# An SSD scan fused with a SiLU feed-forward block: a new order for the first fifty microseconds

## The chip, the cores and the metric

The kernel runs on one core of a Trainium2 chip. The metric is the device time of one execution in microseconds (us); three executions of the kernel before are known, and their median is compared. The engines are named as in the profile: PE is TensorE (PEld its weight loads), DVE VectorE, ACT ScalarE, POOL GpSimd, SP the queue that issues most DMAs. A DMA issued by POOL goes through another queue than those of SP.

## What is computed

Two blocks follow each other. The first is a Mamba-2 state-space scan with batch 4, 8 heads, 768 positions, head size 32 and state size 16; the second a feed-forward block with SiLU on the 3072 x 256 result. Cut to what matters:

```python
log_a = np.log(np.clip(a, 1e-06, 1.0))
for c in range(nc):                                   # chunks of 32 positions
    cum = np.cumsum(la, axis=-1)
    L = np.exp(cum[:, :, :, None] - cum[:, :, None, :]) * causal
    M = np.einsum('bhin,bhjn->bhij', Cc, Bc) * L
    y = np.einsum('bhij,bhjd->bhid', M, xc) + np.einsum('bhin,bhnd->bhid', Cc, state) * np.exp(cum)[..., None]
    state = np.exp(np.sum(la, -1))[:, :, None, None] * state + (decayed sum of B x over the chunk)
x = attn_out.transpose(0, 2, 1, 3).reshape(B * S, H * D)   # 3072 x 256
h = x @ w_in                                               # 256 x 2048
return (h * (1.0 / (1.0 + np.exp(-h)))) @ w_out            # 2048 x 256
```

## The kernel before

The work on tokens is cut into twelve *units* of 256 positions (three to a batch), each in four chunks of 64. The weights come in sixteen *blocks* of 128 x 512: 0 to 7 of w_in, 8 to 15 of w_out. Blocks are counted from zero here and in the code, so the "blocks six, seven" of the change's short name are blocks 5 and 6 of this text.

The weights arrive as pairs of 32-bit words (`load_w`, a tile `raw`, one of six buffers of the pool `quad`), and are made into float32 on the chip. `w_size(n)` on ACT writes `wu` with an Abs (L189) and `wv` with a scaled copy (L192). `w_bits(n)` on DVE clamps `wu` (a Max and a Min, L203), shifts it (L205) and puts the sign into `wv` (L206); POOL adds the two into the block `w` (L208). With `parts=2` the add is done in two halves, so that a product can start on the first.

For each unit the scan goes like this. `f_Ab` (unit 0 to 1) spreads the decays with PE into PSUM; `f_Ek` and `f_E1` make the decay matrix E from them by a running product on DVE (L358, the "scan"); later units load `ab` by DMA and scan from SBUF. `f_P` makes the prefix products `pfx` (L350) from `pz`, which POOL clips (`f_P0`, L346) for units 0 to 2. `f_TP` transposes B and C on PE (L396) and copies them out as BH (L399) and CT (L402) on ACT; `f_T` does it by a DVE transpose (L387); `f_T2` makes CE, two masked copies of C (L409, ACT). `f_B` and `f_C` weight B and C (L382, L413). `f_G` and `f_D0` are the score and state products on PE (L443, L429), `f_M` multiplies scores by E (L449, DVE), `f_S` carries the states on (L463, DVE), `f_SM` masks them (L470, ACT), `f_Y` makes y on PE (L483, L492), and `f_X` copies it out as `xf` (L502, ACT). E has one buffer, so a unit's scan waits for the y of the unit ahead; the PSUM tile `gy` (four banks) is one buffer too, and the banks of `acc` and `half` are two each.

Units 0 and 1 go through the feed-forward block in plain float32: `f_s1(u, j)` is unit u's product with block j into one of two PSUM halves `hp` (L532), with the Silu on ACT (L535, `gT`) that frees it; `f_s2(j)` is the product with block 8 + j (L545). From then on the units go in pairs through a split form (float32r, a high part, a low part and a cross term: L560, L568, L609, L610, L640), which fills the rest of the kernel. DMAs with accumulation from POOL make the low parts of the weights (L219, L229).

The order is written out by hand: the program runs under a manual schedule, so each engine and each queue executes its own operations in the order in which the Python code emits them, and waits by semaphores. The change lies in the list of calls from L697 to L782 and in the table `steps` (L841), which interleaves products, scans and weight blocks: an entry `(1, 4, "b7 r13 s8")` is unit 1's product with block 4, then `w_bits(7)`, the load of block 13 and `w_size(8)`; in "2:DSsM" the letters stand for parts of unit 2's scan (T: transposes and CE, P: prefix products, 1 and 2: the halves of E, B, C, D: the score and state products, S, s, M, Y: y and xf, x and a: loads). `busy` puts idle products on PE as filler.

Of the kernel before, what the change touches and what calls it, by code (L numbers as in the profile page):

```python
# [33 lines left out]
def kernel(  # L34
# [61 lines left out]
    def acc(name):  # L96
        return ps_a.tile([128, 512], FP32, name=name, tag="a")
# [18 lines left out]
    def load_n(u, i, q, ks=(0, 1)):  # L116
        b, t0 = at(u)
        if i == 1:
            if u not in tbc:
                tbc[u] = block("tbc0")[:, 0:256].rearrange("p (k h n) -> p k h n", k=2, h=H)  # L120
        elif u not in bn:
            bn[u] = (block("bn0")[:, 0:256].rearrange("p (k h n) -> p k h n", k=2, h=H) if u in (0, 1, 3) else
                     loads.tile([128, 2, H, N], FP32, name="bn"))
        for k in ks:
            q.dma_start(out=(bn, tbc)[i][u][:, k], in_=(B, C)[i][b, :, t0 + 128 * k:t0 + 128 * k + 128].rearrange("h p n -> p h n"))
# [49 lines left out]
    def load_w(n, q):  # L175
        j = n % 8
        src = wi[:, :, j * WF:(j + 1) * WF] if n < 8 else wo[:, 2 * j:2 * j + 2]
        if src.dtype == FP32:
            w32[n] = block("w32")
            q.dma_start(out=two(w32[n]), in_=src)  # L180
            return
        t = raw[n] = quad.tile([128, 2, WF, 2], U32, name="raw", tag="quad")
        q.dma_start(out=t.rearrange("p k f two -> p k (f two)"), in_=src.bitcast(U32))
# [10 lines left out]
    def w_bits(n, parts=1):  # L194
        if n in raw:
            u, v, hi = two(wu.pop(n)), two(wv.pop(n)).bitcast(U32), raw[n][:, :, :, 1]
            w32[n] = block("w32")
            for i in range(parts):
                fs = slice(WF // parts * i, WF // parts * (i + 1))
                if i == 0 or n == 0:  # L200
                    ws = fs if n == 0 else slice(0, WF)
                    ui = u[:, :, ws].bitcast(U32)
                    nc.vector.tensor_scalar(out=u[:, :, ws], in0=u[:, :, ws], scalar1=LEAST, scalar2=MOST,  # L203
                                            op0=ALU.max, op1=ALU.min)
                    nc.vector.tensor_scalar(out=ui, in0=ui, scalar1=3, scalar2=None, op0=ALU.logical_shift_left)  # L205
                    nc.vector.scalar_tensor_tensor(out=v[:, :, ws], in0=hi[:, :, ws], scalar=0x80000000, in1=v[:, :, ws],  # L206
                                                   op0=ALU.bitwise_and, op1=ALU.bitwise_or)
                nc.gpsimd.tensor_tensor(out=two(w32[n])[:, :, fs].bitcast(U32), in0=u[:, :, fs].bitcast(U32),  # L208
                                        in1=v[:, :, fs], op=ALU.add)
# [88 lines left out]
    def busy(n, small=0, t=None):  # L298
        t = half("zero") if t is None else t
        for i in range(n):  # L300
            nc.tensor.matmul(out=t, lhsT=idle[:, 0:128], rhs=idle, start=True, stop=True)
        for i in range(small):
            nc.tensor.matmul(out=t[:64, :64], lhsT=idle[:, 0:64], rhs=idle[:, 64:128], start=True, stop=True)
# [87 lines left out]
    def f_TP(u):  # L391

        d = new_dp(u)
        for i, t in enumerate((bn[u],) if u == 0 else (bn[u], tbc.pop(u))):
            for k in range(2):
                nc.tensor.transpose(out=d[:, 2 + i, 256 + 128 * k:384 + 128 * k],  # L396
                                    in_=t[:, k].rearrange("p h n -> p (h n)"), identity=ident)
        BH[u] = sc.tile([128, UT], FP32, name="bh")
        nc.scalar.activation(BH[u], d[:, 2, 256:512], AF.Copy)  # L399
        if u == 1:  # L400
            CT[u] = sc.tile([128, UT], FP32, name="ct")
            nc.scalar.activation(CT[u], d[:, 3, 256:512], AF.Copy)  # L402
        elif u > 0:
            CT[u] = d[:, 3, 256:512]

    def f_T2(u, e):
        if e == 0:
            CE[u] = sc.tile([128, 2, UT], FP32, name="ce")
        nc.scalar.activation(CE[u][:, e], CT[u], AF.Copy, scale=par[:, e:e + 1])  # L409
# [6 lines left out]
    def new_dp(u):  # L416
        if u not in DP:
            DP[u] = bank4()
        return DP[u]
# [285 lines left out]
    f_T(0, 1)  # L705
    for e in range(2):
        f_T2(0, e)
    load_w(4, nc.sync)
    load_ab(2, nc.sync)
    load_a(2)  # L710
    f_A1()
    f_Ek(0, 0, slice(4, 8))
    f_Ek(0, 1, slice(0, 4))
    busy(1, 10, new_dp(0)[:, 0])
    f_G(0)
    f_Ek(0, 1, slice(4, 8))
    f_B(0)
# [17 lines left out]
    busy(2)  # L735
    f_X(0)
    load_n(2, 1, nc.gpsimd, (0,))
    w_bits(1, 2)
    load_n(2, 1, nc.gpsimd, (1,))
    w_size(2)  # L740
    f_s1(0, 0)
    w_size(3)
    w_bits(2, 2)
    f_s1(0, 1)
    f_TP(1)
    for e in range(2):
        f_T2(1, e)
    f_Ek(1, 0)
    load_bcx(3, "c")
    for n in range(5, 7):  # L750
        load_w(n, nc.sync)
    f_Ek(1, 1)
    f_B(1, nc.gpsimd)
    f_s1(0, 2)
    w_bits(3, 2)
    w_size(4)
    f_P0(1, nc.gpsimd)
    f_G(1)
    f_D0(1)
    w_bits(4, 2)  # L760
# [5 lines left out]
    f_A2(True)  # L766
    f_A2(False)
    f_A3()
    load_w(7, nc.sync)
    load_pa(3, nc.sync)  # L770
    f_S(1)
    f_SM(1)
    f_M(1, 0)
    f_M(1, 1)
    f_s1(0, 3)
    w_size(5)
    f_s1(0, 4)
    f_Y(1)
    f_X(1)
    w_size(6)  # L780
    w_bits(5)
    load_n(3, 0, nc.gpsimd)  # L782

    def stage(u, what):
        for c in what:
            if c == "L":
                load_unit(u)
            elif c == "a":
                load_ab(u + 1, nc.sync)
            elif c == "x":  # L790
                load_x(u, nc.gpsimd)
            elif c == "T":
                if 0 < u < UPB:
                    f_TP(u)
                else:
                    f_T(u, 0)
                    f_T(u, 1)
                f_T2(u, 0)
                f_T2(u, 1)
            elif c == "P":  # L800
                f_P(u)
            elif c in "12":
                f_E1(u, int(c) - 1, 2)
            elif c == "B":
                f_B(u)
            elif c == "C":
                f_C(u)
            elif c == "D":
                f_G(u)
                f_D0(u)  # L810
            elif c == "M":
                f_M(u, 0)
                f_M(u, 1)
            elif c == "S":
                f_S(u)
            elif c == "s":
                f_SM(u)
            elif c == "Y":
                f_Y(u)
                f_X(u)  # L820
            elif c == "h":
                f_xh(u)
            elif c == "l":
                f_xl(u)
            elif c == "d":
                f_xd(u)
# [4 lines left out]
    def todo(text):  # L831

        for step in text.split():
            if ":" in step:
# [3 lines left out]
            n = int(step[1:].split(".")[0])  # L838
            {"b": w_bits, "s": w_size, "h": w_h, "l": w_l, "d": w_d, "v": partial(w_d, vector=True), "m": f_s2, "p": s1_d, "r": load_r}[step[0]](n)

    steps = ((1, 0, "2:PT1"), (1, 1, "2:C2Ba r8 r9 r10"), (1, 2, "3:x b6 r11 s7"), (1, 3, "2:DSsM r12"),  # L841
             (1, 4, "b7 r13 s8"), (0, 5, "3:T s9"), (1, 5, "2:Y b8 r14"), (0, 6, "3:1PC s10"),
             (1, 6, "b9 r15 3:2B s11 h0 l0"), (0, 7, "2:h s12"), (1, 7, "3:D b10 3:SsM"))
    for u, j, text in steps:
# [119 lines left out]
```

## Time and profile before

| what | us |
|---|---|
| median of three executions (333.96, 334.64, 336.03) | 334.64 |
| the profiled execution's own time | 334.75 |
| its span, from the first to the last instruction | 333.0 |
| clock granted to PE | 1.00 |
| DVE, ACT and POOL busy, share of the span | 76%, 66%, 28% |

How to read it: the timeline view gives, for each row, the start in the span, the time, the engine, the line, the operation with its tiles, and how many were merged; a bracket at the end gives the idle time of the engine before the row and what released it. Rows of issued DMAs (`DMA_DIRECT2D`) give the time of the issue, not of the transfer; the trace gives the time to landing for those of POOL. The chain of waits follows the work that ended last backwards, to what released each step. The DMA share is the mean busy share of the core's sixteen DMA engines.

Some rows of the first 50 us: unit 0's y ends at 13.62 and unit 1's at 29.89; unit 1's scans on DVE run from 18.34 to 20.66 behind blocks 1 and 2, beside POOL's adds of block 2 (18.73 to 20.16); block 5's DVE operations run from 30.36 to 32.96, unit 2's first scan from 33.91 to 36.14; SP issues blocks 5 and 6 at 26.09, the write of a_in at 32.44, block 7 at 34.02, unit 3's pz at 34.53, its ab at 37.61, and blocks 8 to 15 from 38.96 to 53.5.

### The profile page before, as it was taken

The page shows a single profiled execution, that of the slowest core. Times are in us where ns is not written, and L with a number is a line of the kernel's source. Part 1 is how long each engine was busy: PE and PEld are TensorE (multiplying, and loading weights), DVE is VectorE, ACT ScalarE, POOL GpSimd, SP SyncE. Part 2 cuts the span into 40 slices and gives each one's busy share as a digit, 9 for nine tenths or more (in the row PEclk, how much of TensorE's full clock was granted, in tenths as well). Part 3 has the DMA queues.
Part 4 walks back from the last instruction along what each step waited for, and adds up shares of the span by engine and source line. Part 5 has one row for each costly group of instructions (what it writes and reads, how often), then busy time and mean ns, then how long its engine had stood idle before and what let it go on. Part 6 is the DMA issues. An engine that isn't in the chain of part 4 may idle for free.

```text
span 333.0 us, 7980 instructions
## 1 busy us (share of the span) xinstructions
PE 322.2 (97%) x3219; PEld 260.3 (78%) x3221; DVE 253.3 (76%) x413; ACT 220.4 (66%) x422; POOL 92.5 (28%) x96
## 2 busy tenths in 40 slices
PE   8986989999999999999999999999999999999995
PEld 4565877888878778778778778778778778899995
DVE  7897979986876987996875996875996863484443
ACT  3665558687488898666767676767666756656661
POOL 6779735477011222231202230202240202000000
PEclk9999999999999999999999999999999999999999
DMA  6966796867893683164510254510253000012001
GB/s 138 291 172 194 196 368 212 161 111 126 147 172 76 116 150 63 49 110 90 107 31 0 54 106 93 112 23 0 60 101 64 2 2 0 0 27 39 0 2 63
DMA packets 79700, 31.87 MB, mean 96 GB/s; under 512 B 63168, under 2 KB 70080, under 8 KB 79664
## 3 DMA queue, kind: packets, MB, share of 16 engines
q1 hardware_dynamic: 73856, 24.42, 31.8%
q0 software_dynamic: 3440, 6.56, 10.5%
q10 hardware_dynamic: 2368, 0.39, 0.6%
q8 instruction: 25, 0.41, 0.5%
q14 instruction: 11, 0.09, 0.1%
HBM read 22.79 MB, written 3.32 MB: 78 GB/s over the span
## 4 chain that ended last, share of the span: by engine, by line
PE 88%; DMA 8%; ACT 2%; SPq 1%; issue 0%; DVE 0%
PE hp L568 23%; PE hp L560 11%; PE oa L609 9%; PE oa L610 9%; PE b L640 9%; PE oa L545 8%; PE hp L532 3%; DMA a_first<-ach 3%; PE b L635 2%; PE b L618 2%; PE oa L618 2%; DMA raw<-in_moe_w_out_dram 2%; PE gy L492 2%; PE gy L443 2%; DMA ab<-a_first 2%; PE gy L483 2%
## 5 line engine op out<-in xcount | busy, mean ns | idle before, releaser
L562 ACT ACTIVATE hp<-hp 128x512 f32<-128x512 f32 x80 | 46.6, 582 | 70.4 <-PE hp L560 70.3
L582 DVE TENSOR_TENSOR gl<-g,gh 128x512 fp32r<-128x512 f32 x62 | 42.7, 689 | 50.8 <-ACT gh L578 47.8
L568 PE MATMUL hp<-xh,wh 128*128 128x512 f32 x160 | 65.4, 409 | 0.0
L586 DVE SCALAR_TENSOR_TENSOR gd<-gh,g 128x512 fp32r<-128x512 f32 x80 | 59.5, 747 | 5.2 <-ACT gh L578 5.2
L582 POOL TENSOR_TENSOR gl<-g,gh 128x512 fp32r<-128x512 f32 x18 | 29.2, 1621 | 121.9 <-ACT gh L578 121.9
L568 PE MATMUL hp<-xl,wl 128*128 128x512 f32 x160 | 62.8, 392 | 0.0
L578 ACT ACTIVATE gh<-g 128x512 fp32r<-128x512 f32 x80 | 50.6, 632 | 2.7
L609 PE MATMUL oa<-gh,wh 128*128 128x512 f32 x128 | 50.0, 391 | 0.0
L610 PE MATMUL oa<-gl,wl 128*128 128x512 f32 x128 | 50.0, 391 | 0.0
L560 PE MATMUL hp<-xd,wd 128*128 128x512 f32 x160 | 49.6, 391 | 0.0
L576 ACT ACTIVATE g<-hp 128x512 f32<-128x512 f32 x80 | 47.4, 593 | 0.6 <-PE hp L568 0.6
L568 PEld LDWEIGHTS hp<-xh,wh 128*128 128x128 f32 x160 | 30.1, 188 | 8.8 <-ACT hp L562 2.5
L532 PE MATMUL hp<-xf,w 128*128 128x256 f32 x128 | 30.4, 387 | 5.8 <-POOL w L208 2.5
L560 PEld LDWEIGHTS hp<-xd,wd 128*128 128x128 f32 x160 | 30.0, 188 | 6.8
L640 PE MATMUL b<-gd,wd 128*128 128x512 f32 x128 | 34.6, 390 | 0.0
L568 PEld LDWEIGHTS hp<-xl,wl 128*128 128x128 f32 x160 | 30.1, 188 | 4.8
L532 PEld LDWEIGHTS hp<-xf,w 128*128 128x128 f32 x128 | 23.2, 190 | 11.5 <-POOL w L208 4.5
L358 DVE TENSOR_TENSOR_SCAN E<-ab,diag 128x512 f32<-128x512 f32 (+1 forms) x26 | 29.6, 1166 | 0.8 <-PE ab L365 0.6
L208 POOL TENSOR_TENSOR w<-wu,wv 128x512 uint32<-128x512 uint32 (+1 forms) x21 | 25.1, 1206 | 17.3 <-DVE wv L206 17.2
L545 PE MATMUL oa<-gT,w 128*128 128x256 f32 x128 | 28.8, 381 | 0.0
L609 PEld LDWEIGHTS oa<-gh,wh 128*128 128x128 f32 x128 | 24.0, 188 | 5.2
L640 PEld LDWEIGHTS b<-gd,wd 128*128 128x128 f32 x128 | 24.0, 188 | 5.1
(105 smaller groups left out, 476.2 us busy)
## 6 DMA issues: line engine op xcount, KB each, us to landing
ab<-a_zero SPq DMA_DIRECT2D x18, 256.0 KB
raw<-in_moe_w_in_dram SPq DMA_DIRECT2D x8, 512.0 KB
raw<-in_moe_w_out_dram SPq DMA_DIRECT2D x8, 512.0 KB
wl<-w POOLq DMA_DIRECT2D x16, 256.0 KB, 3.8
out_dram<-ot SPq DMA_DIRECT2D x40, 64.0 KB
xt<-in_x_dram SPq DMA_DIRECT2D x19, 128.0 KB
tbc<-in_C_dram SPq DMA_DIRECT2D x40, 32.0 KB
pz<-a_in SPq DMA_DIRECT2D x9, 130.0 KB
```

The lines of the kernel that those rows point to most:

```text
L532: nc.tensor.matmul(out=hp[:, i], lhsT=two(w32[j])[:, kc, 128 * i:128 * i + 128], rhs=two(XF[u])[:, kc], start=(kc == 0), stop=(kc == KC - 1))
L545: nc.tensor.matmul(out=OA[0][m][:, UT * u:UT * u + UT], lhsT=two(w32[8 + j])[:, i, 128 * m:128 * m + 128], rhs=two(GT[u, j])[:, i], start= ...
L560: nc.tensor.matmul(out=HP[s], lhsT=two(WD[f // 2])[:, kc, 128 * (f % 2):128 * (f % 2) + 128], rhs=XD[P][:, kc], start=(kc == 0), stop=Fals ...
L562: nc.scalar.activation(HP[s], HP[s], AF.Copy, scale=HALF / UP)
L568: nc.tensor.matmul(out=HP[s], lhsT=two(w[f // 2])[:, kc, 128 * (f % 2):128 * (f % 2) + 128], rhs=x_[P][:, kc], start=False, stop=(kc == KC ...
L576: nc.scalar.activation(G[s], HP.pop(s), AF.Silu, scale=UP)
L578: nc.scalar.activation(GH[s], G[s], AF.Copy, scale=DOWN)
L582: engine.tensor_tensor(out=GL[s], in0=G[s], in1=GH[s].bitcast(FP32), op=ALU.subtract)
L586: nc.vector.scalar_tensor_tensor(out=GD[s], in0=GH[s].bitcast(FP32), scalar=1.0 + 1.0 / HALF, in1=G.pop(s), op0=ALU.mult, op1=ALU.subtract)
L609: nc.tensor.matmul(out=OA[P][m], lhsT=two(WH[n])[:, r, ms], rhs=gh, start=(f == 0), stop=False)
L610: nc.tensor.matmul(out=OA[P][m], lhsT=two(WL[n])[:, r, ms], rhs=gl, start=False, stop=(f == NF - 1))
L640: nc.tensor.matmul(out=B2[P][:, m], lhsT=two(WD[n])[:, r, 128 * m:128 * m + 128], rhs=gd, start=(fresh and s == tiles[0]), stop=True, skip ...
```

## The change

Only the order of operations changes, and the bank that one filler writes. On ACT, unit 0's CE goes ahead of its BH, block 4's Abs and copy go ahead of the Silu of unit 0's third product, block 5's go behind unit 1's xf, and block 6's behind unit 2's CE. On DVE, unit 1's two scans go between blocks 0 and 1 and between blocks 1 and 2, and unit 2's prefix products and first scan go ahead of block 5. On POOL, unit 1's clip goes ahead of block 3's adds. On SP, block 7 is loaded behind 5 and 6, ahead of the writes of a_in, and blocks 8 and 9 ahead of unit 3's pz and ab. Unit 3's B load is emitted in another step of the table, but keeps its place in POOL's order.

```diff
@@ f_TP @@
         BH[u] = sc.tile([128, UT], FP32, name="bh")
-        nc.scalar.activation(BH[u], d[:, 2, 256:512], AF.Copy)
+        if u > 0:
+            nc.scalar.activation(BH[u], d[:, 2, 256:512], AF.Copy)
@@ the list of calls @@
     for e in range(2):
         f_T2(0, e)
+    nc.scalar.activation(BH[0], new_dp(0)[:, 2, 256:512], AF.Copy)
     load_w(4, nc.sync)
...
-    busy(1, 10, new_dp(0)[:, 0])
+    busy(1, 10, acc("zero"))
...
     load_n(2, 1, nc.gpsimd, (0,))
+    f_Ek(1, 0)
     w_bits(1, 2)
     load_n(2, 1, nc.gpsimd, (1,))
     w_size(2)
     f_s1(0, 0)
     w_size(3)
+    f_Ek(1, 1)
     w_bits(2, 2)
     f_s1(0, 1)
     f_TP(1)
     for e in range(2):
         f_T2(1, e)
-    f_Ek(1, 0)
     load_bcx(3, "c")
-    for n in range(5, 7):
+    for n in range(5, 8):
         load_w(n, nc.sync)
-    f_Ek(1, 1)
     f_B(1, nc.gpsimd)
-    f_s1(0, 2)
+    f_P0(1, nc.gpsimd)
     w_bits(3, 2)
     w_size(4)
-    f_P0(1, nc.gpsimd)
+    f_s1(0, 2)
     f_G(1)
...
     f_A3()
-    load_w(7, nc.sync)
+    for n in range(8, 10):
+        load_w(n, nc.sync)
     load_pa(3, nc.sync)
...
     f_M(1, 1)
+    f_P(2)
     f_s1(0, 3)
-    w_size(5)
     f_s1(0, 4)
     f_Y(1)
     f_X(1)
-    w_size(6)
-    w_bits(5)
-    load_n(3, 0, nc.gpsimd)
+    w_size(5)
@@ stage @@
+            elif c == "n":
+                load_n(u, 0, nc.gpsimd)
@@ steps @@
-    steps = ((1, 0, "2:PT1"), (1, 1, "2:C2Ba r8 r9 r10"), (1, 2, "3:x b6 r11 s7"), (1, 3, "2:DSsM r12"),
+    steps = ((1, 0, "2:T1 b5 s6"), (1, 1, "2:C2Ba r10"), (1, 2, "3:nx b6 r11 s7"), (1, 3, "2:DSsM r12"),
```

## The prediction

> **What bounds the kernel now.** I read three views in this order: the busy table of the page, the timeline of each engine over the first 52 us, and the chain of waits over the same stretch. The busy table says that there is little to win.
>
> ```profile
> PE 322.2 (97%) x3219; PEld 260.3 (78%) x3221; DVE 253.3 (76%) x413; ACT 220.4 (66%) x422; POOL 92.5 (28%) x96
> ```
>
> TensorE is idle for 333.0 - 322.2 = 10.8 us of the span. Its timeline has no gap of note after 50.48 us, so everything there is to win lies ahead of that, and a gain there reaches the end one for one unless a later supplier is late.
>
> ```profile
> 7.67 0.38 PE L301 MATMUL gy<-misc 128*128 128x512 bf16 x1 [0.47 <-ACT bh L399]
> ...
> 17.05 2.00 PE L532 MATMUL hp<-xf,w 128*128 128x256 f32 x8 [0.68 <-POOL w L208]
> ...
> 23.22 2.00 PE L532 MATMUL hp<-xf,w 128*128 128x256 f32 x8 [0.70 <-POOL w L208]
> 26.30 1.99 PE L532 MATMUL hp<-xf,w 128*128 128x256 f32 x8 [1.08 <-POOL w L208]
> ...
> 31.68 1.99 PE L532 MATMUL hp<-xf,w 128*128 128x256 f32 x8 [1.79 <-ACT xf L502]
> 33.51 0.38 PE L396 MATMUL gy<-ident,bn 128*128 128x128 f32 x2
> ```
>
> The bracket is the idle time before the row and who ended it. With 0.16 at 13.78, 1.09 at 48.15 and 0.36 at 50.48 these gaps add up to 6.3 us. The last row has no bracket: the transposes of unit 2 follow at once. The chain of waits says why ScalarE is late twice.
>
> ```profile
> 26.09 3.54 DMA raw<-in_moe_w_in_dram
> 29.64 0.02 issue
> 29.66 0.66 ACT wu L189
> 30.32 0.55 ACT wv L192
> 30.87 0.48 ACT gT L535
> 31.35 0.28 ACT xf L502
> ...
> 38.96 7.30 DMA raw<-in_moe_w_out_dram
> 46.26 0.02 issue
> 46.28 0.03 ACT wu L189
> ```
>
> The Abs of block 5 and of block 8 stand in ScalarE's order ahead of Silus that TensorE needs, and wait for their blocks to land (29.64 and 46.26). The first holds up unit 1's x copy (L502), the second the Silu that frees the PSUM half for the 48.15 product.
>
> **The change, queue by queue.** TensorE keeps its order; only the filler writes another bank. GpSimd's order differs in one place: unit 1's clip (0.45 us) goes ahead of block 3's adds. VectorE, ScalarE and SP are reordered.
>
> CE ahead of BH, filler in another bank. CT is ready at 5.12 + 0.61 = 5.73, so CE (0.90) is done at 6.6, while BH still runs from 7.24 to 7.62. The filler follows the transposes at 7.2 and takes 8.48 - 7.67 = 0.81, so the scores start at 8.00 and not at 8.46: 0.46 gained, which unit 0's chain through VectorE, x copy and block 0's adds carries to 13.7 (first scan slot 13.72 for 14.18). The bank that the filler takes was read by a scan ending at 5.20: no new wait.
>
> Scans between the blocks. Each scan is 2.32 / 2 = 1.16 us. Moved ahead, they delay block 1 by one scan and block 2 by two; nothing is added. What it may save is collisions: block 1 took 1.82 us and block 2 2.34, against 1.39 (42.39 to 43.78) for a block with GpSimd quiet, while the two scans and GpSimd's two adds of 18.73 ran side by side at 1.16 and 0.72 each. It also makes a new collision: block 1's Max (L203) now falls into the C load that GpSimd issues behind block 0's adds (0.91). The row for that is block 5's.
>
> ```profile
> 30.36 0.73 DVE L203 TENSOR_SCALAR wu<-wu 128x512 f32<-128x512 f32 x1 [2.10 <-ACT wu L189]
> 31.12 0.84 DVE L205 TENSOR_SCALAR wu<-wu 128x512 uint32<-128x512 uint32 x1
> ```
>
> Both are 0.41 and 0.43 elsewhere; here each ends 0.25 behind one of the two x loads that GpSimd issued from 29.95 (ends 30.83 and 31.71). I walk both ways. With the collision: block 1 14.86 to 16.83, scan to 17.9, block 2 (behind block 1's adds and the second C load) to 20.1, block 3 to 22.4, block 4 to 24.4. Without: 16.3, 17.4, 19.1, 21.1, 23.4. In the profile shown block 4 ended at 25.05. So TensorE first loses: block 1's product starts at 17.6 (17.05), block 2's at 21.1 (19.52), block 3's at 24.1 (23.22); then, since block 4's Abs now stands ahead of a Silu, block 4's at 26.0 (26.30). Without the collision these are 17.05, 19.9, 22.8 and 24.65. The prefix scan, states and mask products of unit 1 keep their 3.21 us (25.05 to 28.26): ready at 27.6 or 26.6.
>
> The Trainium skill, page "SBUF — State Buffer", section "Who interferes with whom", and its box on DMAs from the GpSimd queue, have it that a two-port VectorE operation holds the port that GpSimd needs for writing descriptors, so that the DMA is what waits, if VectorE was first. By that reading the walk without the collision holds, and the sum below would be 2.5 us; with the collision it is 1.5.
>
> Abs of blocks 5 and 6 behind unit 1's y. ScalarE no longer waits for 29.64 between two Silus. Unit 1's y then ends at 29.35 (28.05 without the collision) and not 29.89, its x copy follows within 0.6 us, and unit 1's first product starts at 29.9 (28.6) instead of 31.68: the 1.79 gap becomes some 0.55, a gain of 1.8 to 3.1 at this point. Behind the moved Abs waits only the next Silu, due at 31.9 and again two products later; the block landed at 29.64.
>
> What is late next. Unit 2's transposes follow that product at 31.9 (30.6) and need unit 2's B, which GpSimd issues behind unit 1's cw, itself behind block 4's adds and unit 1's prefix scan.
>
> ```profile
> 26.90 0.68 POOL L413 TENSOR_TENSOR cw<-ct,pfx 128x256 f32<-128x256 f32 x1
> 27.66 0.40 POOL L346 TENSOR_SCALAR pz<-pa 128x256 f32<-128x256 f32 x1
> 28.12 1.83 POOL L125 DMA_DIRECT2D bn<-in_B_dram  x2
> ```
>
> The second of the two, at 29.07, landed 3.8 us later, at 32.87; the weight load of these transposes began at 33.30. So this load is only 0.43 us behind being the bound, and it moves with VectorE: 4.02 us after the start of the prefix scan, so issued at 28.4 with the collision and 27.4 without. Its flight is the unknown: 3.8 in its own row, 4.5 for its twin while blocks 5 and 6 filled the queues (DMA share 1.00 from 28 to 30 us), 5.1 for an x load beside weight blocks at 37.67, 6.7 for C loads among everything at 10 to 13 us. With block 7 now issued right behind 5 and 6, the weight traffic lasts 1.6 us longer; I take 4.8, between the second and the third row, which are nearest in what flies beside it. For the issue I take 28.0, between the two walks, since the collision has a row on either side: beside the accumulating DMA of 62.41 the same two operations took 0.41 and 0.43. So it lands near 32.8, a gain of 0.5 at the transposes. The ends: 27.4 + 3.8 = 31.2, a gain of 2.1; 28.4 + 6.7 = 35.1, a loss of 1.8.
>
> Unit 2's scan ahead of block 5. Both VectorE operations fill the 2.10 us in which it waited for block 5's Abs; the second needs E free (unit 1's y, 29.35) and ends at 30.6, when that Abs is done. Zero; without that cover it would be 1.16 + 0.69 on block 5, which its product at 42 us (add done near 34) would still not see.
>
> SP's order. Block 7's load (0.40 to issue) now precedes the writes of a_in, which wait for GpSimd until 32.44 anyway: zero on SP. Blocks 8 and 9 precede pz of unit 3 and ab of unit 3. In the profile shown block 8 stood behind ab, which waited for VectorE's last scan of unit 2 until 37.6; now it is issued near 33.5 and, even at 7.30, lands at 40.8, before its Abs is due (42.8). So both gaps at 48.15 and 50.48 go: 1.09 + 0.36 = 1.45. pz and ab come 0.9 later at most in the queue and are read at 49.5 and 48.4; both are covered by over 5 us. Unit 3's B load moves behind later work of other queues, but not in GpSimd's order: zero.
>
> After 50 us. The next products need block 8 (48.57 + 2.12 = 50.7, used 56.87), xd of unit 3 (72.88, used 75.54) and WD of block 0 (landed 72, used 75.54). All of these suppliers hang on the same chain and start earlier with it, so the 2.7 to 6 us of cover hold.
>
> **Sum.** 0.5 at the transposes (all the gains and losses before them end there) plus 1.45 behind them = 1.95 us. The profiled execution took 334.75 us (span 333.0 and 1.75 around it), 0.1 over the median of 334.64. 334.75 - 1.95 = 332.8.
>
> **The rivals.**
>
> Larger gain: no collision, and B flies 3.8 to 4.5, or lands before it is needed. For it: 18.34 to 20.66, where scans and adds ran freely. Against: the 30.36 row. Gain at the transposes 1.4 (27.4 + 4.5) to 2.7 (30.6, with no wait for B), in all 2.9 to 4.1: 330.6 to 331.9.
>
> Slower: unit 2's B lands late, since block 7's 512 KB now share its flight. It decides at 33.30 + 1.45 = 34.75, that is a flight of 6.3 us from 28.4. At 7.7 (the first B load from GpSimd, issued at 7.65) it lands at 36.1: a loss of 2.8 against the gain of 1.45, so 336.1. For it: that row and the 6.7. Against: those had three times as many transfers ahead of them; the twin beside two blocks took 4.5.
>
> The change doesn't do what it says at block 8: the Silu before 48.15 stays late, since ScalarE now has block 6's Abs behind unit 2's CE and block 7's later. Then 0.5 is left: 334.2. Against: I find these done by 36.2 and 39.2, with Silus due at 36 and 39.
>
> **How the numbers follow.** Forecast 0.48 (332.0 to 333.7: flights of 4.5 to 5.1 from either issue, and 0.2 more), larger gain 0.26, block 8 unchanged 0.11, slower 0.15. The first three reach from 330.6 to 334.2, the slower one from 334.7 up; leaving out the end of the larger gain, some 0.08, and the far part of the slower one, some 0.10, the range is 330.9 to 335.3. One per cent, about what a measurement can tell from no change, is 331.3 and 338.0: somewhat over half of the larger gain lies below 331.3, 0.15; no mechanism above passes 338.0, but a later stage that I took as covered may, 0.08; within one per cent is the rest, 0.77.
>
> **What would show it.** Right: scores of unit 0 at 8.0; block 1's to 3's products later than 17.05, 19.52 and 23.22; unit 1's first product near 30; a new gap of about a microsecond before unit 2's transposes, ended by a DMA of bn, and they start near 32.8; no gap from there to the end, block 8's Abs not waiting. Wrong: transposes without a gap (larger gain), or after 34.7 (slower); a Silu ending a gap near 46; a new gap behind 52 us, which would mean that a supplier I called covered is not.

## The result

| | before | after |
|---|---|---|
| median, us (20 executions each, on the same chip) | 334.67 | 336.46 |
| range, us | 333.06 to 336.55 | 334.73 to 338.85 |
| span and own time of the profiled execution, us | 333.0, 334.75 | 334.8, 336.49 |
| clock granted to PE in it | 1.00 | 0.995 |

The ratio is 1.0053, 95% interval [1.0033, 1.0072]: half a per cent slower, 1.8 us. The forecast was 332.8 us, a gain of 1.95. What happened is the rival "slower": unit 2's B lands late. It stood at 336.1 us with a chance of 0.15. The ratios here and below are estimates over the fast executions of both kernels, and can differ by some 0.2% from the quotient of the two medians.

The page of the changed kernel, busy time and granted clock (its lines from L399 on have moved by one, so L532 is L533 here):

```profile
PE 322.5 (96%) x3219; PEld 261.0 (78%) x3221; DVE 251.8 (75%) x413; ACT 220.9 (66%) x422; POOL 92.0 (27%) x96
...
PEclk9999799999999999999999999999999999999999
```

PE's busy time is within 0.3 us of the 322.2 before, and one slice of the clock line, the fifth of forty (33.5 to 41.9 us), is at 7 tenths. TensorE's timeline before, at three places that change:

```profile
33.95 5.35 PE L532 MATMUL hp<-xf,w 128*128 128x256 f32 x24
...
48.15 1.97 PE L532 MATMUL hp<-xf,w 128*128 128x256 f32 x8 [1.09 <-ACT gT L535]
50.48 5.45 PE L532 MATMUL hp<-xf,w 128*128 128x256 f32 x24 [0.36 <-ACT gT L535]
```

And of the changed kernel:

```profile
7.18 0.70 PE L444 MATMUL gy<-ce,bh 32*64 32x128 f32 x32 [0.23 <-ACT bh L709]
...
17.12 1.99 PE L533 MATMUL hp<-xf,w 128*128 128x256 f32 x8 [1.66 <-POOL w L208]
...
20.39 2.00 PE L533 MATMUL hp<-xf,w 128*128 128x256 f32 x8 [0.84 <-POOL w L208]
...
23.72 4.20 PE L533 MATMUL hp<-xf,w 128*128 128x256 f32 x16 [0.32 <-POOL w L208]
...
29.99 1.99 PE L533 MATMUL hp<-xf,w 128*128 128x256 f32 x8 [0.47 <-ACT xf L503]
35.61 0.77 PE L396 MATMUL gy<-ident,bn 128*128 128x128 f32 x2 [3.63 <-DMA bn<-in_B_dram]
36.17 0.64 PE L396 MATMUL gy<-ident,tbc 128*128 128x128 f32 x2
36.60 6.51 PE L533 MATMUL hp<-xf,w 128*128 128x256 f32 x24
...
50.80 7.17 PE L533 MATMUL hp<-xf,w 128*128 128x256 f32 x32
57.91 0.69 PE L444 MATMUL gy<-ce,bh 32*64 32x128 f32 x32
```

Unit 1's first product starts at 29.99 behind a gap of 0.47, where before it started at 31.68 behind 1.79. Then TensorE stands still for 3.63 us until unit 2's B has landed, and starts the transposes at 35.61 (33.51). The gaps that stood at 48.15 and 50.48 are gone: 32 products run as one from 50.80. Two things ahead of that row are slower: the transposes take 0.77 and 0.64 (0.38 each before), the 24 products 6.51 (5.35). The table by stretches says why (columns: stretch; length; busy time of PE, PEld, DVE, ACT and POOL, with counts; granted clock; DMA share; GB/s):

```profile
34.00:36.00 2.00, 0.39 (x2) 0.28 (x3) 0.00 (x0) 0.00 (x0) 2.00 (x3) 0.88 1.06 252
36.00:38.00 2.00, 2.00 (x8) 1.73 (x8) 0.01 (x1) 1.16 (x4) 2.00 (x3) 0.50 1.05 372
38.00:40.00 2.00, 2.00 (x9) 1.69 (x8) 1.97 (x4) 1.37 (x3) 0.17 (x1) 0.76 0.99 267
```

In the trace's clock records TensorE had half its clock from 35.53 for 3.41 us, which costs an estimated 3.41 x 0.5 = 1.7 us of work. The chain of waits goes through the landing, as the rival had it:

```profile
27.74 7.73 DMA bn<-in_B_dram
35.61 1.19 PE gy L396 x4
36.81 6.30 PE hp L533 x24
```

One caution about all starts: they count from the first instruction, and inputs do not arrive equally soon. Unit 0's transposes stood at 6.81 in the execution of before and at 5.92 in that of after (at 5.50 to 6.81 in all sixteen profiles), so up to 0.89 us of an "earlier" can be arrival. Counted from those transposes:

| from unit 0's transposes to | before | after | difference |
|---|---|---|---|
| unit 1's first product | 24.86 | 24.06 | -0.80 |
| unit 2's transposes | 26.70 | 29.69 | +2.99 |
| unit 2's scores | 32.41 | 37.11 | +4.70 |
| unit 3's scores | 49.04 | 51.99 | +2.95 |
| end of the span | 326.22 | 328.86 | +2.64 |

The steps between the rows are the story: 0.80 won up to unit 1's first product, 3.79 lost at the landing, 1.71 at half clock, 1.75 won back where the two gaps were. 2.64 less the 0.89 of earlier arrival is the 1.8 of the two spans; that the medians differ by as much does not follow from it, since arrival and clock change from execution to execution. The count also takes off too much where the weights set the pace: unit 1's first product stood at 30.00 with unit 0's transposes at 5.77, and only 0.42 later with them 0.87 later (6.64), in two kernels below that have the same order up to there.

### The profile page after: what moved, and what is told of

The parts are those of the page before. It is cut to its first block, busy times and chain, and to the rows that moved or that the text cites. A ratio compares the mean times of both kernels' runs of the same rounds, so it can differ in the third digit from the quotient of the medians.

```text
span 334.8 us, 7981 instructions
## 1 busy us (share of the span) xinstructions
PE 322.5 (96%) x3219; PEld 261.0 (78%) x3221; DVE 251.8 (75%) x413; ACT 220.9 (66%) x422; POOL 92.0 (27%) x96
## 4 chain that ended last, share of the span: by engine, by line
PE 90%; DVE 3%; POOL 3%; DMA 2%; issue 1%; POOLq 0%; DVEq 0%
PE hp L569 23%; PE hp L561 11%; PE oa L610 9%; PE oa L611 9%; PE b L641 9%; PE oa L546 8%; PE hp L533 6%; PE gy L493 2%; PE b L636 2%; DMA bn<-in_B_dram 2%; PE b L619 2%; PE oa L619 2%; PE gy L444 2%; POOL w L208 2%; PE gy L484 2%; PE gy L430 1%
## 5 line engine op out<-in xcount | busy, mean ns | idle before, releaser
L533 PE MATMUL hp<-xf,w 128*128 128x256 f32 x128 | 31.3, 397 | 3.7 <-POOL w L208 2.8
L533 PEld LDWEIGHTS hp<-xf,w 128*128 128x128 f32 x128 | 24.4, 197 | 9.2 <-POOL w L208 5.2
L208 POOL TENSOR_TENSOR w<-wu,wv 128x512 uint32<-128x512 uint32 (+1 forms) x21 | 24.3, 1165 | 21.0 <-DVE wv L206 18.4
L611 PEld LDWEIGHTS oa<-gl,wl 128*128 128x128 f32 x128 | 24.0, 188 | 5.1
```

The source lines that it names most:

```text
L533: nc.tensor.matmul(out=hp[:, i], lhsT=two(w32[j])[:, kc, 128 * i:128 * i + 128], rhs=two(XF[u])[:, kc], start=(kc == 0), stop=(kc == KC - 1))
L611: nc.tensor.matmul(out=OA[P][m], lhsT=two(WL[n])[:, r, ms], rhs=gl, start=False, stop=(f == NF - 1))
```

## The experiments

Theory A: block 7's 512 KB, now ahead of unit 2's B, make it land late. Theory B: the new order on DVE (unit 2's scan ahead of block 5) does. Theory C: the scans between the blocks make the issue of unit 2's B late. Each run is the changed kernel with one edit, if nothing else is said; medians go against the kernel before on the same chip: 335.76 in the first group, then 334.92, 335.27 and 335.15.

**Block 7's load put back behind the writes of a_in**

```diff
-    for n in range(5, 8):
+    for n in range(5, 7):
...
-    for n in range(8, 10):
+    for n in range(7, 10):
```

> Block 7's load goes back behind the writes of a_in; all else as in the changed kernel. Theory A (unit 2's B flies 7.2 to 7.7 us because block 7's 512 KB are queued ahead of it, and the idle TensorE then drops its clock): flight back to about 4.5 us, transposes of unit 2 near 32.5 to 33, granted clock 1.00 throughout, 332.5 to 333.5 us, ratio to the kernel before near 0.996. Theory B (VectorE's prefix products and scan, moved into the time in which GpSimd writes descriptors, hold the flight up): flight stays over 7 us, transposes after 35, 336.5 us. Theory C (the later blocks 1 to 3 carry through to unit 2): 336 or more, with a B issued as late as now.

335.73 us, ratio 0.9991 [0.9968, 1.0015]. TensorE's timeline:

```profile
33.58 0.43 PE L396 MATMUL gy<-ident,bn 128*128 128x128 f32 x2 [1.58 <-DMA bn<-in_B_dram]
...
48.46 0.34 PE L493 MATMUL gy<-E,xt 64*32 64x64 f32 x14 [1.40 <-issue]
48.73 8.86 PE L533 MATMUL hp<-xf,w 128*128 128x256 f32 x32
```

The transposes start 2.03 us earlier and the half clock behind them is gone: theory A holds. But a new pause of 1.40 us stands inside unit 2's y, with no releaser ("issue"), and behind it the clock is halved for 3.41 us: the 32 products take 8.86 in place of 7.17. So only part of the gain is seen in the time (the changed kernel's ratio is 1.0053). Of the twelve executions six have a mean clock of 0.994 or 0.995, the others 1.00.

**Unit 2's prefix products and scan back behind block 5**

```diff
-    f_P(2)
     f_s1(0, 3)
...
     w_size(5)
+    w_bits(5)
...
-(1, 0, "2:T1 b5 s6")
+(1, 0, "2:PT1 s6")
```

> Unit 2's prefix products and first scan go back behind block 5 on VectorE; block 7 stays where the change put it. Theory A: flight of unit 2's B still over 7 us, transposes after 35, 336 to 337 us. Theory B: flight about 4.5 us, transposes near 33, 333 to 334 us.

336.89 us, ratio 1.0029 [1.0012, 1.0046]. Both halves of unit 2's B are late, whatever DVE does first; theory B falls:

```profile
34.65 0.30 PE L396 MATMUL gy<-ident,bn 128*128 128x128 f32 x1 [2.66 <-DMA bn<-in_B_dram]
35.48 0.33 PE L396 MATMUL gy<-ident,bn 128*128 128x128 f32 x1 [0.54 <-DMA bn<-in_B_dram]
```

**Unit 1's scans back behind block 2**

```diff
-    f_Ek(1, 0)
     w_bits(1, 2)
...
-    f_Ek(1, 1)
     w_bits(2, 2)
...
         f_T2(1, e)
+    f_Ek(1, 0)
+    f_Ek(1, 1)
```

> Unit 1's two scans go back behind block 2 on VectorE; all else as in the changed kernel. Theory A: products of blocks 1 to 3 start up to 1 us earlier than in the changed kernel, but the flight of unit 2's B stays over 7 us and with it the transposes after 35: 336 to 337 us. Theory C: the transposes start 1 us or more earlier, 335 us or less.

336.59 us, ratio 1.0017 [0.9993, 1.0042]. B is issued at 26.89 (27.74), 0.43 earlier when counted from unit 0's transposes, and the wait is hardly shorter:

```profile
33.84 0.30 PE L396 MATMUL gy<-ident,bn 128*128 128x128 f32 x1 [2.71 <-DMA bn<-in_B_dram]
34.67 0.36 PE L396 MATMUL gy<-ident,bn 128*128 128x128 f32 x1 [0.53 <-DMA bn<-in_B_dram]
```

Theory C falls as the cause: an earlier issue behind the same three blocks lands nearly as late.

**Fourteen idle products in the wait**, so that TensorE is busy while B is late (a step "f" ahead of unit 2's transposes):

```diff
+            elif c == "f":
+                busy(14, 0, acc("zero"))
...
-(1, 0, "2:T1 b5 s6")
+(1, 0, "2:fT1 b5 s6")
```

> The changed kernel with 14 idle products (about 3 us) on TensorE between unit 1's first product and unit 2's transposes, where it now waits 3.6 us. The transposes can't start earlier than now (35.5), so what changes is the clock alone. If the drop to half clock behind the wait is a price of its own: clock 1.00, 1.7 us back, 334.5 to 335. If not (the time is set by the late B alone): 336.5 as now. If the filler runs longer than the wait: up to 1 us more.

335.5 us, ratio 0.9981 [0.9964, 0.9998].

```profile
31.98 2.97 PE L301 MATMUL zero<-misc 128*128 128x512 bf16 x13
34.90 0.63 PE L396 MATMUL gy<-ident,bn 128*128 128x128 f32 x2
...
35.59 5.35 PE L533 MATMUL hp<-xf,w 128*128 128x256 f32 x24
```

The records show 13 of the 14. The 24 products are back at 5.35. B is still late (flights of 6.5 to 7.1 us), and yet the ratio falls to 0.9981, from 1.0053 for the changed kernel and from 1.0029 and 1.0017 for the two runs of the same group whose B is late and whose clock drops (DVE order back, scans back): the price of the half clock, seen apart. Ten of the twelve executions have a mean clock of 0.998 or more, against three of 20 of the changed kernel. That the kernel ends level with the one before owes something to the latter, which had a mean clock under 0.997 in 34 of its 35 executions on this chip.

**B by SP's queue**, ahead of unit 3's B and C and of the blocks:

```diff
+    load_n(2, 0, nc.sync)
     load_bcx(3, "c")
...
-    load_n(2, 0, nc.gpsimd)
```

> Unit 2's B is issued by SP ahead of unit 3's B and C, some 5 us earlier, and no longer by GpSimd; block 7 and all else as in the changed kernel. Theory A: the wait of 3.6 us before unit 2's transposes goes, they start at 32.0, right behind unit 1's first product, with no clock drop there: span near 331, 332 to 333 us, ratio to the kernel before near 0.991, unless the x of unit 2 (also in flight with block 7) is the next to be late, which would show as a gap before the state products near 38. Rival (the early lateness of blocks 1 to 3 decides): transposes at 32 and yet 334 or more.

332.94 us, ratio 0.9942 [0.9916, 0.9967]. B is issued at 23.17 and the transposes follow the product without a bracket, block 7 again standing right behind 5 and 6:

```profile
13.71 2.06 PE L533 MATMUL hp<-xf,w 128*128 128x256 f32 x8 [0.37 <-ACT xf L503]
17.58 1.99 PE L533 MATMUL hp<-xf,w 128*128 128x256 f32 x8 [1.80 <-POOL w L208]
...
20.85 2.00 PE L533 MATMUL hp<-xf,w 128*128 128x256 f32 x8 [0.84 <-POOL w L208]
...
24.17 4.20 PE L533 MATMUL hp<-xf,w 128*128 128x256 f32 x16 [0.32 <-POOL w L208]
...
30.44 1.99 PE L533 MATMUL hp<-xf,w 128*128 128x256 f32 x8 [0.47 <-ACT xf L503]
32.27 0.38 PE L396 MATMUL gy<-ident,bn 128*128 128x128 f32 x2
```

**The same with the scans back, and the blocks ahead of unit 3's B and C**

```diff
+    f_Ek(1, 0)
+    f_Ek(1, 1)
+    load_n(2, 0, nc.sync)
     for n in range(5, 8):
         load_w(n, nc.sync)
+    load_bcx(3, "c")
```

> As e5_b_by_sp, and unit 1's scans back behind block 2, and blocks 5 to 7 issued ahead of unit 3's B and C. Theory A with the scans as a loss of 0.85 us: transposes near 31, 0.8 us less than e5_b_by_sp, 331.5 to 332.3 us. If the scans between the blocks are a gain once B is on time: 0.5 us or more above e5_b_by_sp.

332.24 us, ratio 0.9918 [0.9886, 0.995]. It can't be told apart from the run ahead of it. Its one new wait is for VectorE, which had itself waited 3.13 us for unit 3's ab to land:

```profile
54.30 0.46 PE L430 MATMUL gy<-xt,BT 64*32 64x64 f32 x32 [0.97 <-DVE BT L382]
```

**Block 7 and the scans both put back**

> Both undone in the changed kernel: block 7's load behind the writes of a_in, unit 1's scans behind block 2; B still issued by GpSimd. Theory A: B issued at 26.9 and 27.9 as in e4_scans_back, flight 5.0 to 5.7 as in e1_block7_back, so transposes near 33.0 (33.58 in e1_block7_back); 0.6 us less than e1_block7_back without its stall near 47: 333 to 334 us.

335.98 us, ratio 1.0008 [0.9974, 1.0041]. The profiled execution took 331.71 us:

```profile
32.42 0.46 PE L396 MATMUL gy<-ident,bn 128*128 128x128 f32 x2 [0.61 <-DMA bn<-in_B_dram]
```

One other took 332.25; the other ten took 335.7 to 337.5, at a mean clock of 0.989 to 0.995 against 0.998. None of those ten was profiled.

**The kernel before with only blocks 8 and 9 earlier**, that is one part of the change alone:

```diff
-    load_w(7, nc.sync)
+    for n in range(7, 10):
+        load_w(n, nc.sync)
...
-"2:C2Ba r8 r9 r10"
+"2:C2Ba r10"
```

> The kernel before with one part of the change: blocks 8 and 9 issued ahead of unit 3's pz and ab. By the prediction's term: transposes stay at 33.5, the gaps at 48.15 and 50.48 go, 1.45 us less than the kernel before. If these gaps have another cause (the Silus behind them stay late): no difference.

336.14 us, ratio 1.0022 [0.9994, 1.005]. In the profiled execution (333.9 us) the gaps at 48.15 and 50.48 are gone, and half of their 1.45 us comes back as the pause inside unit 2's y. The median shows no gain at all; eight of the twelve executions have a mean clock of 0.99 to 0.995, the profiled one 1.00:

```profile
47.96 0.34 PE L492 MATMUL gy<-E,xt 64*32 64x64 f32 x14 [0.71 <-issue]
48.23 7.17 PE L532 MATMUL hp<-xf,w 128*128 128x256 f32 x32
```

**The kernel before with only block 7 earlier**

```diff
-    for n in range(5, 7):
+    for n in range(5, 8):
         load_w(n, nc.sync)
...
-    load_w(7, nc.sync)
```

> The kernel before with one edit: block 7's load is issued right behind blocks 5 and 6, ahead of the writes of a_in; nothing else moves. Theory A (block 7's 512 KB lengthen the flight of unit 2's B): B is issued as before (28.1 and 29.1), flies 6.5 to 7.5 us instead of 3.8 to 4.5, unit 2's transposes start at 35.6 to 36.6 instead of 33.51 behind a gap of some 2.4 us that ends with a DMA of bn, perhaps with the half clock behind it; 336.5 to 338.5 us, ratio 1.005 to 1.011. Rival D (block 7 alone is harmless, it needs the earlier scans or blocks of the change to make B late): the transposes start within 0.3 us of 33.51, ratio 0.999 to 1.001.

335.45 us, ratio 1.001 [0.9989, 1.0031], as rival D had it; the profiled execution is the slowest of the ten (337.46). The flight is as theory A had it, 7.0 us in place of 4.1, but the gap expected at the transposes is not there:

```profile
33.00 3.78 PE L532 MATMUL hp<-xf,w 128*128 128x256 f32 x8 [3.89 <-ACT xf L502]
36.58 0.63 PE L396 MATMUL gy<-ident,bn 128*128 128x128 f32 x2
```

Here block 5 was issued a microsecond later (27.09) and its Abs, in the old order, holds up unit 1's x copy, so that the product starts at 33.00; B's landing hides behind that. In the old order of Abs a late B cost little here, since TensorE was late itself.

**The kernel before with only B by SP**

```diff
+    load_n(2, 0, nc.sync)
     load_bcx(3, "c")
...
-    load_n(2, 0, nc.gpsimd)
```

> The kernel before with one edit: unit 2's B is loaded by SP ahead of unit 3's B and C, and not by GpSimd. It tells what of the gain of the changed kernel with B by SP (0.994) belongs to the change. Theory A: before, TensorE does not wait for B at the transposes (31.68 to 33.51 is the product behind unit 1's x copy), so an earlier B is worth nothing there: transposes within 0.3 us of 33.5, gaps of 1.1 and 0.4 us near 48 and 50.5 stay, ratio 0.998 to 1.002. Rival: the move of the load by itself (less work for GpSimd and its descriptors beside VectorE) is worth the 0.6 per cent, ratio 0.992 to 0.996.

338.72 us, ratio 1.0085 [1.0057, 1.0114]: neither of the two. The edit that gains 0.6% in the changed kernel costs 0.85% here. ScalarE's timeline:

```profile
33.48 0.66 ACT L189 ACTIVATE wu<-raw 128x512 f32<-128x512 f32 x1 [5.58 <-DMA raw<-in_moe_w_in_dram]
```

SP issues block 5 at 28.25 (26.09), behind B and unit 3's B and C, and ScalarE waits for it 5.58 us with a Silu and unit 1's x copy in line behind; unit 1's first product starts at 35.51. The change's order of Abs is what makes an early B worth having.

**Block 7 back, and blocks 10 to 15 one step later**, against the pause of 1.40 us:

```diff
-"2:C2Ba r10", "3:nx b6 r11 s7", "2:DSsM r12", "b7 r13 s8", "2:Y b8 r14", "b9 r15 ...", "m0 b11 ..."
+"2:C2Ba", "3:nx b6 r10 s7", "2:DSsM r11", "b7 r12 s8", "2:Y b8 r13", "b9 r14 ...", "m0 r15 b11 ..."
```

> The run with block 7's load put back, and blocks 10 to 15 are each issued one step of the table later. There the time gained at the transposes was lost again in a pause of 1.40 us inside unit 2's y with no releaser shown. Theory I (TensorE's next instructions are fetched behind the weight traffic of blocks 10 and 11): with that traffic later the pause falls under 0.5 us and the time to 333.0 to 334.5 us, ratio 0.994 to 0.998. Rival II (the pause has another cause): it stays at a microsecond or more, or moves, and the time stays near 335.7, ratio 0.998 to 1.002. Rival III (the later blocks come too late for their Abs): new gaps behind 55 us that end with a block, 336 us or more.

335.25 us, ratio 0.9979 [0.9946, 1.0012], between 332.31 and 337.78. The profiled execution is the slowest of these and has the pause, longer:

```profile
49.84 0.34 PE L493 MATMUL gy<-E,xt 64*32 64x64 f32 x14 [1.84 <-issue]
```

**The same with the scans back too**

> The run with block 7 and the scans put back, and blocks 10 to 15 each one step of the table later. That run took 331.7 us where it was profiled and 335.7 to 337.5 in most executions. Theory I: the slow executions had the pause for instructions inside unit 2's y; without the traffic most executions take 331.5 to 333.5 us, ratio 0.989 to 0.995. Rival II: most stay above 335.5, ratio 0.998 to 1.002. Rival III: later blocks come too late, gaps behind 55 us, 334 to 337 us in all executions.

336.22 us, ratio 1.002 [0.9988, 1.0052]; no gain, and a B that lands late behind two blocks only:

```profile
35.42 0.66 PE L396 MATMUL gy<-ident,bn 128*128 128x128 f32 x2 [3.41 <-DMA bn<-in_B_dram]
...
50.83 0.34 PE L493 MATMUL gy<-E,xt 64*32 64x64 f32 x14 [0.62 <-issue]
```

Moving the blocks does not remove the pause.

**Block 7 back, and six idle products ahead of the transposes**, which put 12 more instructions into TensorE's program:

```diff
+            elif c == "f":
+                busy(6, 0, acc("zero"))
...
-(1, 0, "2:T1 b5 s6")
+(1, 0, "2:fT1 b5 s6")
```

> The run with block 7's load put back, and six idle products between unit 1's first product and unit 2's transposes (0.21 us each, 12 more instructions for TensorE). Theory I, told by position (the pause inside unit 2's y is a wait for a batch of instructions that begins at a fixed place in TensorE's program): the pause moves six products forward, from behind the 50th of 64 to behind the 44th, and if it stays it ends 1.3 to 1.5 us behind the transfer of the instruction packet; 335 to 336 us. Rival II (the pause comes from something in unit 2's y, E or its accumulators): it stays behind the 50th product. Of the clock: the transposes start within 0.4 us of 33.58 and without a gap over 0.5 us before them; if it is the pause that halves the clock, an execution with the pause still has 3.41 us at half clock, one without it has none, 332.5 to 333.5 us.

335.1 us, ratio 1.0 [0.9973, 1.0027].

```profile
34.18 0.47 PE L396 MATMUL gy<-ident,bn 128*128 128x128 f32 x2 [0.85 <-DMA bn<-in_B_dram]
...
46.97 0.69 PE L493 MATMUL gy<-E,xt 64*32 64x64 f32 x44
48.17 0.41 PE L493 MATMUL gy<-E,xt 64*32 64x64 f32 x20 [0.52 <-issue]
```

The pause has moved from behind the 50th product of 64 to behind the 44th: six products, 12 instructions. So it is bound to a place in the program. The clock is not halved in this execution.

**B by GpSimd, but ahead of the weight blocks**, behind the two C loads of unit 1; block 7 stays early:

```diff
     load_n(2, 1, nc.gpsimd, (0,))
+    load_n(2, 0, nc.gpsimd, (0,))
...
     load_n(2, 1, nc.gpsimd, (1,))
+    load_n(2, 0, nc.gpsimd, (1,))
...
-    load_n(2, 0, nc.gpsimd)
```

> The changed kernel with one edit: GpSimd issues the two loads of unit 2's B behind the two C loads of unit 1 (about 15 and 18.6 us), ahead of the weight blocks, and not behind cw (27.7). Block 7 stays early. Theory A' (the landing of B is set by the weight blocks that were issued ahead of it, not by the queue or by B's own time): B lands before 24 us, unit 2's transposes follow unit 1's first product at 32 to 32.6 without a gap, the clock is not halved, 333.0 to 334.5 us, ratio 0.993 to 0.998; block 1's and 2's operations on VectorE lose up to 0.4 us each beside the descriptors. Rival (loads from GpSimd are always late beside weight blocks, wherever they are issued): B still lands behind 33.5, ratio over 1.001.

332.28 us (331.22 to 332.95), ratio 0.9929 [0.9903, 0.9955]. GpSimd's and TensorE's timelines:

```profile
15.53 0.89 POOL L125 DMA_DIRECT2D bn<-in_B_dram  x1
...
19.60 0.88 POOL L125 DMA_DIRECT2D bn<-in_B_dram  x1
```

```profile
30.98 1.99 PE L533 MATMUL hp<-xf,w 128*128 128x256 f32 x8 [0.47 <-ACT xf L503]
32.81 0.38 PE L396 MATMUL gy<-ident,bn 128*128 128x128 f32 x2
```

No wait at the transposes, from the same queue, beside the same early block 7. It is the place of B in the order of issues that decides, not the queue. This version and the two with B by SP beat both kernels; among the three the intervals don't decide.

## Why the prediction was wrong, step by step

**What is late next: the step that failed.** "Its flight is the unknown ... I take 4.8, between the second and the third row, which are nearest in what flies beside it." The two loads flew 7.7 and 7.2 us. The DMA views of 25 to 31 us, before and after (KB of each, median flight in us):

```profile
bn<-in_B_dram POOLq DMA_DIRECT2D x2, 64.0 KB, 4.1
```

```profile
raw<-in_moe_w_in_dram SPq DMA_DIRECT2D x3, 512.0 KB
...
bn<-in_B_dram POOLq DMA_DIRECT2D x2, 64.0 KB, 7.4
```

The second load was forecast to go out at 28.0 and land at 32.8; it went out at 28.70 and landed at 35.9. So 0.7 us of the error is the issue, and 2.4 the flight. The prediction had written the reason down itself, that "the weight traffic lasts 1.6 us longer", and gave it 0.3 us over its twin. And a flight is the wrong quantity to carry over. All profiled executions in which GpSimd issues B behind the blocks:

| run | blocks ahead | first block issued | B issued | flight | transposes behind the wait | that less the first block |
|---|---|---|---|---|---|---|
| before | 2 | 26.09 | 28.12 | 4.1 | no wait | |
| block 7 and scans back | 2 | 25.79 | 27.56 | 4.4 | 32.42 | 6.6 |
| blocks 8, 9 alone | 2 | 26.27 | 27.90 | 5.3 | no wait | |
| block 7 back | 2 | 26.37 | 27.75 | 5.3 | 33.58 | 7.2 |
| block 7 back, six products | 2 | 26.74 | 27.79 | 5.9 | 34.18 | 7.4 |
| block 7 back, blocks later | 2 | 27.32 | 28.17 | 5.8 | 34.50 | 7.2 |
| the same, scans back | 2 | 27.36 | 27.77 | 7.1 | 35.42 | 8.1 |
| scans back | 3 | 26.51 | 26.89 | 6.8 | 34.67 | 8.2 |
| DVE order back | 3 | 27.39 | 27.74 | 6.8 | 35.48 | 8.1 |
| fourteen idle products | 3 | 26.77 | 27.69 | 6.8 | filled | |
| block 7 alone | 3 | 27.09 | 27.34 | 7.0 | no wait | |
| after | 3 | 26.25 | 27.74 | 7.4 | 35.61 | 9.4 |

With two blocks ahead, the flight runs from 4.1 to 7.1 and is the shorter, the longer the blocks have been on their way; counted from the first block the wait ends after 6.6 to 7.4 us, once 8.1. With three it ends after 8.1 to 9.4. Another 512 KB at the 372 GB/s of the stretch from 36 us are an estimated 1.4 us, about that step.

The packet records show the two parts. B's first data moved 2.0 us after its issue before and 4.3 us after it in the changed kernel, but in all twelve executions only when 0.8 to 1.05 MB of the blocks had moved, that is when the two blocks ahead were all but through (once 1.4 MB, with the fourteen idle products). From there GpSimd's queue moved its first 128 KB, as much as the two loads of B, in 0.6 to 1.5 us with two blocks ahead, beside 0.05 to 0.2 MB from SP's queue. With three it took 1.7 to 2.2 us beside 0.37 to 0.56 MB, since block 7 was still under way (again except with the idle products). So in these runs B waits until the first two blocks are nearly through, and the third takes its share behind that.

The Trainium skill, page "DMA: Bandwidth & Descriptors", section "Queues, rings and completion order", has each DMA engine take turns between its queues, packet by packet. The stretch beside block 7 looks like turns. The first one does not, as B moved nothing while the first two blocks did; whether B's packets or the writing of its descriptors waits there, no run here tells.

**The price of the wait.** The forecast priced a late B at its length alone, and so did the rival: 7.7 us of flight and a loss of 2.8 at the transposes. Its landing at 36.1 was near (35.9), its mechanism was right, but it put the clock at nothing: 1.7 us. In the table from unit 0's transposes this is a third of all that was lost. That its 336.1 came so close to 336.46 is therefore partly luck. Of the 20 executions of the changed kernel the three at a mean clock of 1.00 took 334.73 to 335.21, the others, at 0.988 to 0.995, 335.64 to 338.85. The kernel before is not free of such drops: its profiled execution had none, but on the later chips 95 of its 108 executions had a mean clock of 0.989 to 0.995. So the table sets an execution without a drop against one with it, and how much of the 1.8 us between the medians is clock, no run tells.

**Scans between the blocks.** The collision is real: block 1's Max stands at 14.39 and takes 0.81 (0.41), beside the C load of 14.08. The products of blocks 1 to 3 start at 17.12, 20.39 and 23.72. In the run with B by SP, which has the same order up to there but for B's loads and begins nearly as the execution of before does (unit 0's transposes at 6.68), they start at 17.58, 20.85 and 24.17, against 17.6, 21.1 and 24.1 walked with the collision. The prediction's row was not as singular as it says, though: the shift took 0.75 to 0.84 in blocks 1 to 4 of the kernel before, and 0.43 where GpSimd was quiet. B's second load went out at 28.70, 4.56 us after the start of the prefix scan (24.14) and not 4.02, since GpSimd's adds of blocks 3 and 4 last until 26.5; counted from unit 0's transposes its first load was 21.82 against 21.31 before, so nothing was won for B at all. Putting the scans back moved that figure to 21.39, 21.91 and 22.27 in three kernels: no more than executions differ. The skill's page "SBUF — State Buffer", section "Who interferes with whom", lets the first to issue have the port; the load was first, by 0.31 us, and VectorE waited. The reading by which the DMA waits was the wrong one for this pair.

**Abs of blocks 5 and 6 behind unit 1's y.** Right as to the gap: 1.79 became 0.47 (some 0.55 forecast). That the product starts at 29.99 (29.9) is luck, by the early arrival: in the run with B by SP it starts at 30.44, a gain of 1.24 where 1.8 was forecast. Unit 1's y ends there at 29.97, where 29.35 was walked and 29.89 stood before.

**CE ahead of BH.** Right: the scores start at 7.18, which is 8.07 by the arrival of before (8.00 forecast), and at 7.64 in the run with B by SP. It is carried on only where the weights are there: in the execution of after unit 0's first product waits 0.37 for its x copy, since ScalarE has block 1's Abs ahead of that and waits for the block to land, and that product is 0.21 later from unit 0's transposes on. In the run with B by SP it starts at 13.71 (13.7 forecast, 14.18 before).

**SP's order.** Right for blocks 8 and 9: the Abs of block 8 has no wait, and both gaps go.

```profile
46.54 0.68 ACT L189 ACTIVATE wu<-raw 128x512 f32<-128x512 f32 x1
```

"Zero on SP" was true of block 7 and beside the point: what it takes is time of the sixteen DMA engines that B needs. That the gaps go is seen in the traces; blocks 8 and 9 alone show no gain in the median.

**Unit 2's scan ahead of block 5.** Right, zero: it ends at 30.78, ahead of the end of the Abs it would have had to wait for (31.06).

Taken together: in the run with B ahead of the weights unit 2's transposes are 0.69 earlier than before and unit 3's scores 2.11, both from unit 0's transposes (6.80 and 6.81), and it takes 332.28 us where 332.8 was forecast. Behind the transposes that is 1.42 of the forecast 1.45. Ahead of them 0.69 is near the forecast 0.5 by chance: the 0.5 was the landing of B, and with no wait for B the walk with the collision had the transposes at 31.9, 1.6 earlier than before. They start at 32.81, where B's loads stand beside blocks 1 and 2 (block 1's shift takes 0.88, 0.43 in the changed kernel), and at 32.27 with B by SP.

## What to carry to other kernels

A small load issued behind large ones is dated by them: count the bytes ahead of it and the time of their issue, and do not carry a flight over from a row with another queue ahead. When a change frees an engine earlier, the next input has to come earlier too; the same edit for that input cost 0.85% without the change, and with it the kernel was 0.6% faster than before. And when a wait on TensorE grows to two or three microseconds, look whether the clock drops behind it: here that cost another 1.7 us.

## What the runs showed of the hardware

**Half clock behind short waits.** In every case the drop begins at a border of 3.41 us steps in the clock records and lasts one step (two with the waits of 3.89 and 5.68 us). Between 7 and 58 us of the sixteen profiles every step with 2.2 us or more of idle TensorE was followed by half clock. So were the two with a pause of 1.40 and 1.84 us inside unit 2's y, but none of the four with a pause of 0.45 to 0.71 there; and in the execution with the 1.40 neither 1.58 us ahead of the transposes nor 1.80 ahead of block 1's product was. That the pause itself halves the clock is read from these rows; no run took it away alone. The Trainium skill, page "TensorE: Matmul & The Clock Gate", section "HAM oscillation — how this bites in real kernels", warns of idle gaps over some 3.4 us; the window agrees with the 3.41, but here drops followed on less than half of it. What else counts (where the wait lies in the step, how large the products around it are) stays open.

**A wait for instructions.** Each pause inside unit 2's y ends 1.2 to 1.5 us after an instruction packet of 16 KB has landed, by the packet records: 47.17 and 48.46 with block 7 back, 49.56 and 51.00 with the DVE order back, 46.62 and 47.96 with blocks 8 and 9 alone, 48.35 and 49.84, 49.51 and 50.83 with the blocks later, 46.94 and 48.17 with six products. In the other profiles the packet landed 1.4 to 2.8 us ahead of that place in the program, and no pause over 0.11 stands there. With the place moving by just the 12 added instructions, this shows a wait for the next batch of the program. The skill's page "Runtime: NRT & Kernel Launch", section "Instruction fetch mechanics", has blocks of 16 KiB and calls their cost mostly hidden; here it was 0.45 to 1.84 us in six executions. Why the packet comes late in some is not settled: the DMA share is at 1.04 to 1.09 from 42 to 46 or 48 us in all of them, but about as high in executions without a pause, and later weight blocks did not help.

**Open.** What ten of twelve executions with block 7 and the scans back lose against the profiled one: the pause and the clock would be enough for it, but none of those was profiled. What lowers the clock in most executions of the kernel before is open too.
